# The order table of a one-core attention and gated-attention kernel is chosen anew, and every rotating buffer gets a fixed place

## The chip, the cores and the metric

The program runs on one core of one Trainium2 chip. The time is the device time of one execution in microseconds (us); three executions of the kernel before took 452.36, 452.16 and 455.88 us, median 452.36. A further execution was profiled: 453.7 us, of which the profile's span is 451.9 us.

## The reference

Two attentions follow each other. The first, for each of 8 batches and 8 heads (576 positions of 64 values), adds a local part and a coarse part. The second takes that sum as `x` and runs 4 causal attentions (experts) with a gate that keeps the best 2 of 4 at each position.

```python
q_d, k_d, v_d = means of q, k, v over 4 neighbouring positions     # 144 positions
out_up   = repeat(softmax(q_d @ k_d.T / 8) @ v_d, 4)
out_local = softmax(where(|i - j| < 4, q @ k.T / 8, -1e9)) @ v
x = (out_up + out_local) as [batch, 576, 512]
logits = x @ w_gate                                                # best 2 of 4, softmax of those
for e in range(4):
    a = softmax(causal((x @ wq[e]) @ (x @ wk[e]).T / 8))
    out += gate[e] * (a @ (x @ wv[e]) @ wo[e])
```

## The kernel before, in words

Heads go in pairs: a pair fills the 128 partitions, so a batch has 4 units of the first attention. Per unit, stage 1 loads `lq`, `lk` and `lv`, makes the local scores (`sc`, L515), masks and normalises them (`lp`), makes the coarse scores (`scd`, L588) and their softmax (`dp`), transposes both (`tp`, L383), and multiplies by the values (`o`, L650 to L662). The coarse values `vd` are means of `v`: in batch 0 TensorE makes them from `lv` with a pooling matrix (`vd_mm`, L573), later VectorE or GpSimd adds them up from a second load `lr` (L567, L568). The sum `x` is split in two parts, `xh` and `xl`, and so are all weights, so that three passes of the fast matmul type give an fp32 product.

Stage 2 projects `x` to queries, keys (`pj`, L693; the first one by pairs, L708), values and gate logits (`pv`, L739 and L748). Each of the projections of L693 is two operations, 12 matmuls of 320 columns and 12 of 256. Stage 3 makes the causal scores (`sq`, L852), the exponentials (`pr`, L875 and L883), their transposes (`tq`, L383), the product with the values (L966, L970) and the output projection (`po`, L989, L1011), which SyncE stores. Batches overlap: stage 1 of one batch, stage 2 of the one before and stage 3 of the one before that are mixed on all engines.

The mixing is written out by hand. `Plan.op` records each operation with the engines that may run it; `Plan.schedule` then goes through the table `SEQ`: an entry is four times the operation's number plus the index of the engine that runs it, and -1 is a filler, one matmul on zeros (L472) that only keeps TensorE busy. The table is thus the order of every engine's queue and the choice of engine, both. All loads and stores are issued by SyncE in the table's order. Buffers rotate by tag: `Buf.__call__` (L190) asks a tile pool for a tile of that tag with its number of buffers, and the pool picks one. The four halves of PSUM (tag `big`) are the exception: `schedule` gives them out itself, from the list `free`, at the place that was given back first.

Of the kernel before, what the change touches and what calls it, by code (L numbers as in the profile page):

```python
# [7 lines left out]
F32 = mybir.dt.float32  # L8
F32R = mybir.dt.float32r
BF = mybir.dt.bfloat16  # L10
I32 = mybir.dt.int32
# [165 lines left out]
TQ, W = 58, 64  # L177
WT, NQD = 16, 48
# [22 lines left out]
class Plan:  # L201
# [40 lines left out]
    def schedule(self):  # L242
# [8 lines left out]
        for o in out:  # L251
            for b in o.allocs:
                if b.tag == "big":
                    b.at = free.pop(0)
# [876 lines left out]
```

## Time and profile before

| | |
|---|---|
| median of three executions | 452.36 us |
| profiled execution | 453.7 us, span 451.9 us |
| TensorE busy | 441.2 us (98%) |
| VectorE busy | 362.5 us (80%) |
| ScalarE busy | 346.1 us (77%) |
| GpSimd busy | 301.2 us (67%) |
| DMA | 52.70 MB, 38.1% of the 16 engines' time |

PE is TensorE's matmuls, PEld its weight loads, DVE is VectorE, ACT ScalarE, POOL GpSimd, SP SyncE (SPq its DMA issues). Busy time is the time in which at least one instruction of the engine ran; a mean duration of a group can be longer than the engine's advance from one to the next, since neighbours overlap. "Issue" as the cause of an idle time means that the engine waited for nothing that the profile shows.

### The profile page before, as it was taken

The page shows a single profiled execution, that of the slowest core. Times are in us where ns is not written, and L with a number is a line of the kernel's source. Part 1 is how long each engine was busy: PE and PEld are TensorE (multiplying, and loading weights), DVE is VectorE, ACT ScalarE, POOL GpSimd, SP SyncE. Part 2 cuts the span into 40 slices and gives each one's busy share as a digit, 9 for nine tenths or more (in the row PEclk, how much of TensorE's full clock was granted, in tenths as well). Part 3 has the DMA queues.
Part 4 walks back from the last instruction along what each step waited for, and adds up shares of the span by engine and source line. Part 5 has one row for each costly group of instructions (what it writes and reads, how often), then busy time and mean ns, then how long its engine had stood idle before and what let it go on. Part 6 is the DMA issues. An engine that isn't in the chain of part 4 may idle for free.

```text
span 451.9 us, 20317 instructions
## 1 busy us (share of the span) xinstructions
PE 441.2 (98%) x8374; PEld 401.8 (89%) x8375; DVE 362.5 (80%) x1020; ACT 346.1 (77%) x1099; POOL 301.2 (67%) x485
## 2 busy tenths in 40 slices
PE   8998999999999999999999999999999999999997
PEld 4787999989999889998899898999999999998876
DVE  8997989896859999777988999895897768445782
ACT  7985899687968898756867888775997687456783
POOL 6997878768867888665764776765984863304320
PEclk9998999999999999999999999999999999999999
DMA  8966537433344544543334432443272200200113
GB/s 251 281 191 188 169 99 212 123 112 83 89 141 137 155 126 136 158 141 89 113 108 160 118 99 65 133 140 92 62 220 63 70 1 4 80 28 14 52 57 106
DMA packets 44300, 52.70 MB, mean 117 GB/s; under 512 B 4144, under 2 KB 27184, under 8 KB 44208
## 3 DMA queue, kind: packets, MB, share of 16 engines
q1 hardware_dynamic: 44208, 51.40, 38.1%
q8 instruction: 66, 1.08, 1.0%
q14 instruction: 26, 0.21, 0.1%
HBM read 40.90 MB, written 9.44 MB: 111 GB/s over the span
## 4 chain that ended last, share of the span: by engine, by line
PE 87%; DVE 4%; DMA 4%; issue 2%; SPq 1%; ACT 1%; DVEq 0%; ACTq 0%
PE pj L693 20%; PE pv L739 10%; PE po L989 10%; PE sq L852 9%; PE o L966 8%; PE tq L383 6%; PE tp L383 5%; PE sc L515 4%; PE o L650 4%; PE scd L588 3%; DMA lv<-in_v_dram 3%; PE pv L748 2%; PE o L657 2%; PE po L1011 1%; PE o L970 1%
## 5 line engine op out<-in xcount | busy, mean ns | idle before, releaser
L875 ACT ACTIVATE pr<-pr,pst 128x384 f32<-128x384 f32 (+8 forms) x144 | 80.0, 558 | 13.3 <-DVE pst L872 12.6
L883 POOL TENSOR_SCALAR pr<-pr,pst,gt 128x64 f32<-128x64 f32 (+8 forms) x97 | 65.9, 687 | 16.2 <-DVE pst L880 12.0
L693 PE MATMUL pj<-xh,wqk_h 128*128 128x320 f32 (+1 forms) x248 | 74.8, 302 | 0.0
L693 PE MATMUL pj<-xh,wqk_l 128*128 128x320 f32 (+1 forms) x248 | 72.8, 293 | 0.0
L693 PE MATMUL pj<-xl,wqk_h 128*128 128x320 f32 (+1 forms) x248 | 72.7, 293 | 0.0
L872 DVE CUSTOM_DVE_ANT_0 pr<-sq,causal_t 128x384 f32<-128x384 f32 (+8 forms) x144 | 63.8, 484 | 5.2 <-PE sq L852 4.7
L852 PE MATMUL sq<-k,q 64*64 64x256 f32 (+6 forms) x768 | 52.2, 370 | 0.0
L693 PEld LDWEIGHTS pj<-xh,wqk_h 128*128 128x128 f32 x248 | 46.5, 188 | 2.5 <-issue 0.6
L693 PEld LDWEIGHTS pj<-xh,wqk_l 128*128 128x128 f32 x248 | 46.5, 188 | 0.0
L693 PEld LDWEIGHTS pj<-xl,wqk_h 128*128 128x128 f32 x248 | 46.5, 187 | 0.0
L978 POOL TENSOR_TENSOR ol<-oc,oh 128x256 fp32r<-128x256 f32 (+1 forms) x27 | 22.1, 822 | 32.4 <-ACT oh L977 22.6
L852 PEld LDWEIGHTS sq<-k,q 64*64 64x64 f32 x768 | 32.9, 133 | 7.0 <-issue 0.3
L598 ACT ACTIVATE dp<-scd,dst 128x144 f32<-128x144 f32 x96 | 35.2, 376 | 3.4 <-DVE dst L593 2.7
L739 PE MATMUL pv<-wvg_h,xh 128*128 128x260 f32 x128 | 37.0, 289 | 0.0
L739 PE MATMUL pv<-wvg_l,xh 128*128 128x260 f32 x128 | 36.1, 282 | 0.0
L739 PE MATMUL pv<-wvg_h,xl 128*128 128x260 f32 x128 | 36.1, 282 | 0.0
L676 POOL TENSOR_TENSOR xl<-x,xh 128x576 fp32r<-128x576 f32 x22 | 32.4, 1473 | 4.5 <-ACT xh L675 4.0
L536 POOL TENSOR_TENSOR lp<-lp,lst 128x640 f32<-128x640 f32 x24 | 31.9, 1336 | 4.4 <-DVE lst L535 3.7
L383 PE MATMUL tq<-ident,pr 64*128 64x64 f32 x736 | 33.2, 228 | 1.4 <-DVE pst L872 0.6
L989 PE MATMUL po<-oh,wo_h 128*128 128x256 f32 (+1 forms) x112 | 34.0, 304 | 0.0
L989 PE MATMUL po<-oh,wo_l 128*128 128x256 f32 (+1 forms) x112 | 33.0, 294 | 0.0
L383 PEld LDWEIGHTS tq<-ident,pr 64*128 64x128 f32 x736 | 27.1, 138 | 6.5 <-issue 2.6
(182 smaller groups left out, 1438.8 us busy)
## 6 DMA issues: line engine op xcount, KB each, us to landing
lv<-in_v_dram SPq DMA_DIRECT2D x64, 160.0 KB, 3.7
lq<-in_qT_dram SPq DMA_DIRECT2D x32, 292.0 KB, 3.5
lk<-in_kT_dram SPq DMA_DIRECT2D x32, 292.0 KB, 3.9
out_dram<-ot SPq DMA_DIRECT2D x28, 288.0 KB, 2.3
lr<-in_v_dram SPq DMA_DIRECT2D x28, 256.0 KB, 3.2
lr<-in_v_dram SPq DMA_DIRECT2D x56, 32.0 KB, 3.0
wst<-in_wqk_dram SPq DMA_DIRECT2D x1, 1024.0 KB, 9.1
vx<-vg SPq DMA_DIRECT2D x8, 128.0 KB, 2.6
```

Source lines behind the costliest of these rows:

```text
L383: T.transpose(ps()[:, 512 * x + z[x]:512 * x + z[x] + 64], data[r, 0:128], ident[r, r])
L536: op("l_nrm", "GV", (pool_tt(n), dve(n)), lambda e: eng[e].tensor_tensor(p(), p(), st[:, :, 2:3].to_broadcast([128, NT, W]), op=OP.mult), ...
L598: A.activation(p()[:, t, :], scs()[:, at * t:at * t + SD], AF.Exp, bias=st[:, t, 4:5], scale=1.0 / 128.0, accum_out=st[:, t, 0:1])
L676: op("xl", "GV", (1360, dve(576)), lambda e: eng[e].tensor_tensor(xl(), x(), xh()[:, 0:S].bitcast(F32), op=OP.subtract), r=[x, (xh, 0)], w ...
L693: T.matmul(ps()[:, H0 + n0:H0 + n1], ww[:, c, w0 + 128 * p:w0 + 128 * p + 128], xx[b, c]()[:, n0:n1], start=(i == 0), stop=(i == 3 * NP - 1))
L739: T.matmul(ps()[:, at:at + 260], xx[b, c]()[:, 128 * t:128 * t + 128], ww[:, c, :], start=(i == 0), stop=(i == 3 * NP - 1))
L852: T.matmul(pss[x][0]()[halves[e ^ turned(t)], at_of[x] + at + to:at_of[x] + at + to + n1 - n0], q()[r, 64 * t:64 * t + 64], k()[r, n0:n1], ...
L872: op("s_max", "V", dve(n) + 4, lambda x=x, t=t, n=n, src=src: V.tensor_tensor_reduce(rows_of[t], src(), causal_t[:, S - 64:S + 256] if t = ...
L875: op("s_exp", "A", 281 + n / 1.2, lambda x=x, t=t, n=n: A.activation(rows_of[t], rows_of[t], AF.Exp, bias=st[:, x, 4:5], scale=-1.0, accum ...
L883: op("s_nrm", "GV", (327 + n / 1.2 + max(0, n - 384) * 1.1, 189 + n / 1.92), lambda g, x=x, t=t, n=n: eng[g].tensor_scalar(rows_of[t], row ...
L966: T.matmul(obs[x]()[r, q0:q1], vg()[kr, j, 64 * (2 * p + e):64 * (2 * p + e) + 64], pt()[kr, e, j, q0:q1], start=j == 0, stop=j == len(job ...
L989: T.matmul(ps()[:, H1 + n0:H1 + n1], ww[:, p, 128 * c:128 * c + 128], xx[b, p]()[:, n0:n1], start=(i == 0), stop=(i == 5))
```

## The change

The diff has two parts. In the first, every rotating buffer is treated as `big` was: `schedule` keeps a list of free places for each tag, takes the first of it at an allocation and appends a place when its last user has passed, all in the table's order; `Buf.__call__` then asks for a tag with the place's number and one buffer. The constants that are made ahead of the plan name their places too (`up0`, `qd1`, ...).

```diff
-            tag, bufs = (f"big{self.at}", 1) if self.tag == "big" else (self.tag, self.bufs)
-            self.t = self.pool.tile(self.shape, self.dtype, name=self.name, tag=tag, bufs=bufs)
+            self.t = self.pool.tile(self.shape, self.dtype, name=self.name, tag=f"{self.tag}{self.at}", bufs=1)
...
-        free = [1, 2, 3, 0]
+        free = {}
         for o in out:
             for b in o.allocs:
-                if b.tag == "big":
-                    b.at = free.pop(0)
+                b.at = free.setdefault(b.tag, list(range(b.bufs))).pop(0)
             for b in o.bufs:
                 b.left -= 1
-                if b.left == 0 and b.tag == "big":
-                    free.append(b.at)
+                if b.left == 0:
+                    free[b.tag].append(b.at)
...
-    wu = psB.tile([128, 1024], F32, name="wu", tag="big0", bufs=1)
+    wu = psB.tile([128, 1024], F32, name="wu", tag="big3", bufs=1)
```

In the second part the table is another one. It has the same 2562 operations and the same 24 fillers, and its planner counted longer delays for the arrival of instruction blocks. Line numbers after the first hunk fall by 1 or 2.

```diff
 SEQ = (
-    0, 173, 2112, 4, 177, 24, 136, 140, 189, -1, 192, 197, 120, 268, -1, 124, 232, -1, -1, -1, -1, -1, 200, 20,
...
+    214, -1, 156, 160, 288, 292, -1, -1, -1, -1, 296, 220, 8, 417, 12, 180, 164, 168, 73, 185, 320, 324, 248, 216,
...
```

Three places show what the new table moves. The first is TensorE's queue in the first batch, at the third head pair's output; `o` is its accumulator, `pv` the mean values of the fourth pair. Before:

```order
L650 MATMUL o_759<-pt,lv 64x58 x16
L650 MATMUL o_759<-pt,lv 64x56 x4
L573 MATMUL pv<-lv,pool 128x128 x7
L657 MATMUL o_759<-pd,vd 64x144 x4
L660 MATMUL o_759<-pd,vd 64x2x48
L662 MATMUL o_759<-pd,vd 64x48
```

The same place in the change:

```order
L648 MATMUL o_769<-pt,lv 64x58 x16
L648 MATMUL o_769<-pt,lv 64x56 x4
L655 MATMUL o_769<-pd,vd 64x144 x4
L658 MATMUL o_769<-pd,vd 64x2x48
L660 MATMUL o_769<-pd,vd 64x48
L658 MATMUL o_769<-pd,vd 64x2x48
L660 MATMUL o_769<-pd,vd 64x48
L571 MATMUL pv<-lv,pool 128x128 x7
```

The seven long matmuls of `pv` stand behind the short ones of `o` now, not between them.

The second place is the start of SyncE's queue, with the semaphores that each issue waits for (`DMAHW0` to `DMAHW7` are those of the eight DMA lanes that the issues take in turn, `Pool` is GpSimd). Before, from the sixth issue on:

```order
L489 DMA lk_317<-in_kT_dram 128x584
L499 DMA lv_324<-in_v_dram 64x5x128 x2
L488 DMA lq_333<-in_qT_dram 128x584 [waits DMAHW0_49]
L489 DMA lk_405<-in_kT_dram 128x584 [waits DMAHW1_49]
L499 DMA lv_431<-in_v_dram 64x5x128 [waits DMAHW2_49]
L499 DMA lv_431<-in_v_dram 64x5x128 [waits DMAHW3_49]
L488 DMA lq_434<-in_qT_dram 128x584 [waits DMAHW4_49]
L455 DMA wst_527<-in_wqk_dram 128x4x512 [waits DMAHW5_49]
```

In the change:

```order
L494 DMA lr0_95<-in_v_dram 16x512 [waits Pool_49]
L487 DMA lk_324<-in_kT_dram 128x584
L497 DMA lv_326<-in_v_dram 64x5x128
L497 DMA lv_326<-in_v_dram 64x5x128 [waits DMAHW0_49]
L486 DMA lq_363<-in_qT_dram 128x584 [waits DMAHW1_49]
L487 DMA lk_432<-in_kT_dram 128x584 [waits DMAHW2_49]
L486 DMA lq_434<-in_qT_dram 128x584 [waits DMAHW3_49]
L453 DMA wst_519<-in_wqk_dram 128x4x512 [waits DMAHW4_49]
L494 DMA lr1_96<-in_v_dram 16x512 [waits DMAHW5_49,Pool_49]
L497 DMA lv_531<-in_v_dram 64x5x128 [waits DMAHW6_49]
L497 DMA lv_531<-in_v_dram 64x5x128 [waits DMAHW7_49]
```

A small load `lr0`, which needs a tile that GpSimd has filled with zeros, is sixth now, and the second pair's `lv` has moved behind the large weight load `wst`.

The third place is VectorE's queue in batch 6, where it makes the mean values `vd` of the second pair; `oc` is the sum of an output of stage 3. Before:

```order
L327 COPY pd_5987<-tp_5974 128x480
L521 TENSOR_REDUCE lst1_70<-lp_5947 128x10
L676 TENSOR_TENSOR xl_6079<-x_5863,xh_5894 128x576
L567 TENSOR_TENSOR lr1_96<-lr1_96 128x2x256
L568 TENSOR_TENSOR vd_6098<-lr1_96 128x256
L975 TENSOR_TENSOR oc_6102<-o2_6066,oc_6102 128x192
```

In the change:

```order
L973 TENSOR_TENSOR oc_5944<-o2_5921,oc_5944 128x320
L516 SCALAR_TENSOR_TENSOR lp_5952<-sc_5879,lmask_136 128x640
L565 TENSOR_TENSOR lr1_96<-lr1_96 128x2x256
L566 TENSOR_TENSOR vd_5957<-lr1_96 128x256
L881 TENSOR_SCALAR pr20_131<-pr20_131,pst2_77,gt_5984 128x192
L519 TENSOR_REDUCE lst1_70<-lp_5952 128x10
L676 TENSOR_TENSOR xh_5950<-x_5908,xh_5950 128x64
L528 TENSOR_TENSOR lp_5952<-lp_5952,lst1_70 128x640
L325 COPY ptb_6032<-tq_6070 128x2x4x64
```

The two additions for `vd` stand earlier, and the sum `oc` of 192 columns that stood just behind them comes several instructions later.

## Rows read from the trace of the kernel before

**Rows 1.** The page: busy time by engine; 40 slices of PE, PEclk.

```profile
PE 441.2 (98%) x8374; PEld 401.8 (89%) x8375; DVE 362.5 (80%) x1020; ACT 346.1 (77%) x1099; POOL 301.2 (67%) x485
...
PE   8998999999999999999999999999999999999997
...
PEclk9998999999999999999999999999999999999999
```

**Rows 2.** Stretches: length, busy time (instructions) by engine, clock, DMA share, GB/s.

```profile
16.65:37.99 21.34, 17.96 (x525) 15.82 (x525) 18.60 (x40) 19.53 (x64) 20.74 (x25) 1.00 0.76 208
37.99:44.23 6.24, 6.24 (x109) 5.94 (x108) 4.65 (x8) 1.81 (x4) 3.62 (x6) 0.73 0.72 204
39.20:42.60 3.40, 3.40 (x30) 3.18 (x30) 2.93 (x6) 0.78 (x2) 1.45 (x2) 0.50 0.93 281
44.23:441.70 397.47, 395.17 (x7464) 364.60 (x7459) 322.49 (x928) 307.13 (x977) 263.15 (x413) 1.00 0.35 104
```

**Rows 3.** Timeline of PE at two stops: start, length, instruction, idle before.

```profile
21.70 0.40 PE L383 MATMUL tp<-ident,lp 64*128 64x64 f32 x5
23.17 0.40 PE L383 MATMUL tp<-ident,lp 64*128 64x64 f32 x5 [1.07 <-issue]
...
35.27 0.56 PE L515 MATMUL sc<-lk,lq 64*64 64x64 f32 x21
37.50 0.56 PE L515 MATMUL sc<-lk,lq 64*64 64x64 f32 x19 [1.68 <-issue]
```

**Rows 4.** Stretches as Rows 2, from the first stop's end to the second.

```profile
23.10:37.40 14.30, 12.30 (x378) 11.19 (x378) 12.24 (x28) 13.64 (x44) 13.78 (x17) 1.00 0.71 199
```

**Rows 5.** The page's DMA queues: packets, MB, share of 16 engines.

```profile
q8 instruction: 66, 1.08, 1.0%
```

**Rows 6.** Timeline of PE around the second stop, as Rows 3.

```profile
30.70 1.83 PE L573 MATMUL pv<-lv,pool 128*128 128x128 f32 x14
32.46 0.47 PE L657 MATMUL o<-pd,vd 64*64 64x144 f32 x8
...
33.02 0.52 PE L383 MATMUL tp<-ident,lp 64*128 64x64 f32 x10
33.38 0.48 PE L383 MATMUL tp<-ident,dp 64*128 64x64 f32 x10
33.78 0.71 PE L588 MATMUL scd<-kd,qd 64*64 64x144 f32 x12
34.28 0.81 PE L650 MATMUL o<-pt,lv 64*64 64x58 f32 x40
34.90 0.43 PE L657 MATMUL o<-pd,vd 64*64 64x144 f32 x8
...
37.99 0.42 PE L708 MATMUL pj<-xh,wqk_h 128*128 128x320 f32 x1
...
38.90 0.31 PE L708 MATMUL pj<-xh,wqk_h 128*128 128x320 f32 x1
...
40.08 0.47 PE L708 MATMUL pj<-xh,wqk_h 128*128 128x320 f32 x1
...
41.65 0.79 PE L383 MATMUL tp<-ident,lp 64*128 64x64 f32 x10
```

**Rows 7.** Chain that ended last, in order of time: start, length, what.

```profile
49.92 3.17 PE pj L693 x24
...
60.58 1.96 PE pj L693 x12
...
63.31 1.61 PE pj L693 x12
```

**Rows 8.** Timeline of DVE and PE at 270 us.

```profile
270.23 0.86 DVE L676 TENSOR_TENSOR xl<-x,xh 128x576 fp32r<-128x576 f32 x1
271.77 1.00 DVE L567 TENSOR_TENSOR lr<-lr 128x512 f32<-128x512 f32 x1 [0.69 <-DMA lr<-in_v_dram]
272.81 1.38 DVE L568 TENSOR_TENSOR vd<-lr 128x256 f32<-128x256 f32 x1
274.11 0.34 DVE L975 TENSOR_TENSOR oc<-o,oc 128x192 f32<-128x192 f32 x1
...
274.51 0.81 PE L515 MATMUL sc<-lk,lq 64*64 64x64 f32 x40 [0.78 <-DVE oc L975]
```

**Rows 9.** Groups of DVE instructions: shapes xcount, busy us, mean ns, idle before.

```profile
L883 DVE TENSOR_SCALAR pr<-pr,pst,gt 128x576 f32<-128x576 f32 (+7 forms) x47 | 22.4, 491 | 0.7
L551 DVE TENSOR_REDUCE qd<-lq 128x144 f32<-128x576 f32 x19 | 13.9, 731 | 0.1
L568 DVE TENSOR_TENSOR vd<-lr 128x256 f32<-128x256 f32 x11 | 7.3, 666 | 0.4
L334 DVE TENSOR_REDUCE pst<-pst 128x2 f32<-128x4 f32 (+1 forms) x47 | 7.0, 151 | 3.0 <-ACT pr L875 2.8
L327 DVE COPY vg<-pv 128x520 f32<-128x520 f32 x2 | 1.4, 698 | 0.2 <-PE pv L739 0.2
```

**Rows 10.** Stretches of 40 us, as Rows 2.

```profile
40.00:80.00 40.00, 40.00 (x824) 37.58 (x823) 36.34 (x97) 33.78 (x109) 32.70 (x45) 0.97 0.56 168
...
240.00:280.00 40.00, 38.58 (x912) 35.25 (x908) 37.70 (x99) 33.09 (x104) 27.73 (x45) 1.00 0.40 117
```

**Rows 11.** Timeline: GpSimd's preamble; SPq's issues.

```profile
2.82 1.00 POOL L372 TENSOR_SCALAR causal_t<-ci 64x64 bf16<-64x64 int32 x2
...
3.05 0.51 SPq L489 DMA_DIRECT2D lk<-in_kT_dram  x1
...
6.57 1.26 SPq L499 DMA_DIRECT2D lv<-in_v_dram  x2
9.76 0.38 SPq L455 DMA_DIRECT2D wst<-in_wqk_dram  x1
...
20.05 1.72 PE L573 MATMUL pv<-lv,pool 128*128 128x128 f32 x14
```

**Rows 12.** The page's DMA issues: KB each, us to landing.

```profile
wst<-in_wqk_dram SPq DMA_DIRECT2D x1, 1024.0 KB, 9.1
```

More of the change, by code (lines that the diff above doesn't have):

```diff
@@ L298, in tile_attn_then_moe @@
     cst = ctx.enter_context(tc.tile_pool(name="cst", bufs=1))
-    ld = ctx.enter_context(tc.tile_pool(name="ld", bufs=2))
-    wk = ctx.enter_context(tc.tile_pool(name="wk", bufs=2))
+    ld = ctx.enter_context(tc.tile_pool(name="ld", bufs=1))
+    wk = ctx.enter_context(tc.tile_pool(name="wk", bufs=1))
     psB = ctx.enter_context(tc.tile_pool(name="psB", bufs=1, space=bass.MemoryType.PSUM))
@@ L357, in tile_attn_then_moe @@
     V.memset(zero, 0.0)
-    wu = psB.tile([128, 1024], F32, name="wu", tag="big0", bufs=1)
+    wu = psB.tile([128, 1024], F32, name="wu", tag="big3", bufs=1)
     for _ in range(NW0):
         T.matmul(wu[:, 0:512], zero[:, :128], zero, start=True, stop=True)
-    ci = wk.tile([128, 128], I32, name="ci", tag="up")
+    ci = wk.tile([128, 128], I32, name="ci", tag="up0")
     G.iota(ci, pattern=[[1, 128]], base=0, channel_multiplier=-1)
-    cj = wk.tile([128, 128], I32, name="ci", tag="up")
+    cj = wk.tile([128, 128], I32, name="ci", tag="up1")
     G.iota(cj, pattern=[[1, 128]], base=64, channel_multiplier=-1)
-    cut = wk.tile([128, 5, WT], I32, name="cut", tag="qd")
+    cut = wk.tile([128, 5, WT], I32, name="cut", tag="qd0")
     for x, r in enumerate(halves):
@@ L372, in tile_attn_then_moe @@
         G.tensor_scalar(causal_t[x, 512:S], c[x, 0:64], 0.0, 8 * NEG, op0=OP.is_gt, op1=OP.mult)
-    dif2, far = (wk.tile([128, W], F32, name=n, tag=t) for n, t in (("dif", "qd"), ("far", "kd")))
+    dif2, far = (wk.tile([128, W], F32, name=n, tag=t) for n, t in (("dif", "qd1"), ("far", "kd0")))
     for x, c in ((lo, ci), (hi, cj)):
         V.tensor_copy(dif2[x], c[x, 0:64])
-    near = wk.tile([128, W], F32, name="near", tag="kd")
+    near = wk.tile([128, W], F32, name="near", tag="kd1")
     V.tensor_scalar(near, dif2, 0.0, None, op0=OP.is_lt)
@@ L409, in tile_attn_then_moe @@
         V.scalar_tensor_tensor(own[:, x:x + 1], dif2[:, 0:1], -PADL - n + 0.5, own[:, 1:2], op0=OP.is_gt, op1=OP.mult)
-    inside = wk.tile([128, 5, WT], F32, name="inside", tag="vt", bufs=1)
+    inside = wk.tile([128, 5, WT], F32, name="inside", tag="vt0")
     for k0, k1 in ((0, 4), (4, 5)):
```

280 rows, old and new, of the table SEQ are left out of this document.

## The prediction, on record before the run

> **What bounds the kernel now.** I read the page first, then stretches of the span, then the timeline where TensorE stands still. The page says that TensorE's matmuls are busy for 441.2 of 451.9 us and that no slice from the second to the 39th is below eight tenths [rows 1]. The stretches say where the rest is: from 44.23 to 441.70 us PE is busy for 395.17 of 397.47 us, so 397 us of the span hold 2.3 us of visible idle time; from 16.65 to 37.99 us it is busy for 17.96 of 21.34, and behind that the clock falls [rows 2]. The reader should see that this kernel is one TensorE queue with almost no holes. The other engines have at most 80% and matter only where one of them releases a matmul late. Whatever the new table does, it has the same matmuls and the same 24 fillers to run, so it can gain the holes of the first 44 us, the 2.3 us behind them, and small losses at the joints between operations.
>
> **The first part of the change: places.** It costs nothing by itself. I compared the addresses in the program before with a list kept as the change keeps it, first back first taken, over before's own order: of 723 takings of SBUF buffers, some 12 would get another place (6 of `ot`, 2 each of `pt`, `oc` and `dp`). PSUM was given out this way already. So no wait of any weight goes or comes with the places, and the table is the change.
>
> **Term 1, instruction blocks at the head.** TensorE stops twice inside an operation, without any wait: 1.07 us in the middle of ten transposes and 1.68 us in the middle of the 40 local scores [rows 3]. Between the end of the first and the start of the second stand 378 matmuls and 378 weight loads, 756 instructions [rows 4]; with some dozen waits of the sequencer, which that view does not count, this is 768, three times 256. The instruction queue q8 moved 66 packets with 1.08 MB, 16.4 KB each [rows 5], for 8374 + 8375 = 16,749 such instructions [rows 1], 254 a packet. So I read each stop as the start of a packet's instructions that had not arrived. The head is where it can happen: a local score is 40 matmuls and their loads in 0.81 us [rows 8], a pooling (L573) 14 of each in 1.83 us [rows 6].
> The new table moves the last pooling behind the short output matmuls, as the first order piece shows. Counted back from the 1.68 us stop, with a weight load for each matmul, stand 42 instructions of the scores, 32 of the coarse output, 80 of the local output, 24 coarse scores and 40 for two transposes [rows 3, 6]: 218, so some 35 of the packet's 256 are left, the waits taken off. Before, these are the 32 of the coarse output (32.46 to 33.02, 0.56 us) and a few of the pooling; now they are the pooling's 28 (30.70 to 32.46, 1.76 us) and a few of the coarse output [rows 6]. The packet that ends in the stop thus gets 1.0 us more of work to cover the next one's arrival. But the pooling is taken from the packet ahead, which has that much less: the later stop loses some 1.0 us, and 0.5 may come back one packet earlier. I take **-0.5**. The ends: -2.75, if both stops vanish, and +1.07, if one more of the first kind appears.
> On the rule: the Trainium skill, page "Runtime: NRT & Kernel Launch", section "Instruction fetch mechanics", says that instructions come in blocks of 16 KiB, 256 instructions, and that crossing a boundary is mostly hidden because dispatch is slower than the fill. The trace agrees with the size and differs on the hiding: two stops of 1.07 and 1.68 us. By that rule this term would be zero, and so the next.
>
> **Term 2, the clock.** After the second stop the granted clock is 0.50 for 3.40 us, from 39.20 to 42.60, which is 1.2 instead of 2.4 GHz [rows 2]. The first six projection matmuls take 0.91 us (37.99 to 38.90), the twelve after that 2.75 (to 41.65) instead of 1.82 [rows 6]: 0.93 us. The stop of 1.07 us was not followed by such a fall; the stretch from 16.65 to 37.99 has 1.00 [rows 2, 3]. If the second stop shrinks from 1.68 to about 0.7, it is shorter than the one that did no harm. I take **-0.9**; the ends are -0.93 and 0.
>
> **Term 3, joints.** A projection whose two halves follow each other takes 3.17 us; with transposes between them the halves take 1.96 and 1.61, 3.57 in sum [rows 7]. Before, 10 of the query and key projections of L693 are split; now 7. Three joints at 0.2 (half of the 0.40, since the rows' ends are modelled) are **-0.6**; the ends are -1.2 and 0.
>
> **Term 4, VectorE behind a load.** At 271.08 VectorE waits 0.69 us for `lr`, then adds for 2.3 us, and `oc`, next in its queue, comes so late that TensorE stands for 0.78 us [rows 8]. The third order piece moves the additions ahead and puts other work between them and that `oc`. Behind the waiting instruction now stand a normalisation and a maximum of stage 1, whose readers are on other engines. That stop goes, -0.8; but in batch 4 the new table puts three `lr` pieces directly ahead of VectorE's additions, which the old one does not. I take **-0.4**; the ends are -0.8 and +0.8.
>
> **Term 5, VectorE has more to do.** 83 operations go from GpSimd to VectorE and 73 the other way, 45 from ScalarE to VectorE and 33 back. By kinds, VectorE's net gains are 7 normalisations (0.49 us), 8 sums of `qd` and `kd` (0.73), 3 `vd` (0.67 for each of two additions), some 11 evictions (0.70 at most), 3 `o_lo` and 5 `xt`; it loses 11 small sums (0.15), 4 passes over `lp` and one `xl` [rows 9]. With each kind's own mean that is about +16.5 us by durations; durations overlap, so busy time grows by some 15, to 377 of the span, 83%. GpSimd loses about 17. Spread evenly it is 1.3 us in each 40. In the one 40 us stretch behind the head in which VectorE has 37.70, TensorE was idle for 1.42; at 36.34 it was idle for none [rows 10]. So one more stretch, the one at 36.34, comes to 37.7. Half of 1.42 is **+0.7**. The ends are 0 (all of it in VectorE's free time) and +15 (all of it on the path).
>
> **Term 6, loads at the head.** SyncE's sixth issue now waits for GpSimd's zeroed tile. GpSimd is in its preamble until 3.82 and a fill follows, so about 4.3 instead of 3.05 [rows 11]; five earlier transfers are still on their way, so I cost it at nothing. The second `lv` is issued behind the 1 MB weight load, which landed at 9.76 + 9.1 = 18.9 [rows 11, 12]; TensorE asked for that `lv` at 20.05. About a microsecond is left, so **0**; the ends are 0 and +1.
>
> **The sum.** -0.5 - 0.9 - 0.6 - 0.4 + 0.7 = -1.7 us against the profiled execution's 453.7, 452.0 under the profiler. That execution is 1.3 above the median of 452.36; against the median it is 450.7 us. The case's own range, with terms 1, 2 and 4 at either end, is 448.0 to 454.3.
>
> **The rivals.**
> *Blocks don't matter, the head stays as it is.* The stops are of another cause, or spread over other packets at the same sum, and the clock falls as before. Terms 3 to 5 remain: -0.3, **452.1 us**. For it: the dense stretch as a whole holds the same work, only cut otherwise. This is also what the rule of the Trainium skill named above would make of the head. Against it: the 768 instructions between the stops.
> *All stops go.* Both stops, the clock and the 2.3 us behind 44 us: -2.75 - 0.93 - 2.3 - 0.6 = -6.6, **445.8 us**. For it: the table is chosen for longer block delays, and the dense packets later on are thinned too. Against it: the fillers stay and the head's work per packet stays.
> *VectorE becomes the bound.* If its extra work falls into stretches that are full already, half of the 15 us lands on TensorE: +7.5 and terms 1 to 3 at half, -1.0: **458.9 us**. It decides where VectorE passes 37.7 of 40 us in three or more stretches, and TensorE's idle releaser is VectorE. For it: 37.70 in one stretch already. Against it: mean room of 20%.
>
> **How the numbers follow.** Forecast 0.50, head as before 0.22, all stops go 0.15, VectorE bound 0.13. About 1% (4.5 us) is what a measurement here tells from no change. The forecast's own range and the second case lie within it; the third is faster and the fourth slower, and I leave 0.02 of the forecast to each side. Faster 0.17, same 0.68, slower 0.15. Predicted is 450.7; the range takes in the faster case's near half and stops short of the slower one: 446.5 to 457.
>
> **What would show it.** Term 1: the issue stops of PE in the first 40 us, 2.75 in sum, should be about 2.2, none above 1.1. Term 2: no 0.50 clock near 40 us. Term 3: query and key projections with 24 matmuls in one piece, more by three. Term 4: no `DMA lr` wait on VectorE ahead of an `oc` near 270. Term 5: VectorE about 377 us, GpSimd about 285, and PE still idle for under 4 us from 44 us on. Term 6: no PE idle with the second `lv` as releaser. The prediction is wrong if PE's busy time between 44 and 441 us changes by more than 3 us, since nothing above speaks of that.

## The result, and the profile after

The change makes the kernel slower by about half a per cent: 456.86 us, median of 20 executions (454.95 to 461.99), beside 454.21 for the kernel before (also 20 executions); the ratio is 1.0057, 95% interval [1.0038, 1.0077], so 2.6 us with 1.7 to 3.5. The prediction had said 1.7 us faster. The profiled execution of the changed kernel took 454.95 us, the fastest of its 20, so its head is a lucky one; a more usual execution of the same table is profiled below (second run of the experiments).

The page of the changed kernel, busy time, TensorE and its clock in 40 slices:

```profile
PE 442.0 (98%) x8375; PEld 401.0 (88%) x8375; DVE 376.3 (83%) x1054; ACT 341.0 (75%) x1089; POOL 278.5 (61%) x457
...
PE   8989999999999999999899999999999999999997
...
PEclk9999999999999999999999999999999999999999
```

VectorE has 13.8 us more than in [rows 1], GpSimd 22.7 less. Next the stretches, as [rows 2, 10]:

```profile
37.99:44.23 6.24, 6.17 (x165) 5.66 (x165) 5.61 (x11) 4.73 (x16) 5.42 (x8) 1.00 0.73 237
44.23:441.70 397.47, 394.28 (x7386) 363.30 (x7387) 335.36 (x957) 300.79 (x963) 242.37 (x390) 1.00 0.35 103
...
80.00:120.00 40.00, 39.03 (x832) 35.44 (x834) 36.76 (x107) 32.46 (x104) 27.13 (x43) 1.00 0.39 113
200.00:240.00 40.00, 38.61 (x667) 35.98 (x666) 37.33 (x99) 28.19 (x90) 18.82 (x35) 1.00 0.39 114
240.00:280.00 40.00, 40.00 (x928) 36.84 (x928) 35.58 (x101) 32.57 (x102) 28.62 (x46) 1.00 0.43 125
```

In this execution the clock does not fall behind 38 us. The loss of TensorE's busy time sits in two stretches (0.97 and 1.39 us idle), and the stretch from 240 to 280, which idled 1.42 us before, is full now. What TensorE waited for (total us, times, longest):

```profile
PE tq L381 <- DVE pr L881: 1.9, 2, 1.4
...
PE o L660 <- issue: 0.9, 1, 0.9
...
PE sq L850 <- DVE ptb L325: 0.6, 1, 0.6
PE pv L571 <- issue: 0.5, 1, 0.5
PE pj L691 <- DVE x L668: 0.4, 1, 0.4
PE sc L513 <- issue: 0.4, 1, 0.4
```

Three new waits for VectorE, and smaller "issue" stops than in [rows 3]. To see where the time goes I took the start of each TensorE operation in two traces and subtracted. Negative is earlier than in the profiled execution before (us); "new table" is the second run below, "old table" the first:

| at | changed kernel | new table, usual execution | old table, another execution |
|---|---|---|---|
| 56 | -0.8 | +0.75 | +0.4 |
| 110 | +0.7 | +2.3 | +0.4 |
| 190 | +0.8 | +2.3 | +0.6 |
| 240 | +2.6 | +4.0 | +0.6 |
| 300 | +0.9 | +2.3 | +0.6 |
| 435 | +1.3 | +2.8 | +1.25 |

The head differs from execution to execution. The body hardly does (the old table's second execution loses 0.4 us at 344 without a wait): both executions of the new table lose 1.5 us between 56 and 110, 1.7 to 1.8 between 190 and 240, and gain 1.7 between 240 and 300. The place at 220 us, VectorE and GpSimd from 215.4 to 220.6, by form (busy us, mean ns):

```profile
L976 DVE TENSOR_TENSOR ol<-oc,oh 128x320 fp32r<-128x320 f32 x1 | 1.7, 1699 | 0.0
L674 POOL TENSOR_TENSOR xl<-x,xh 128x576 fp32r<-128x576 f32 x1 | 1.6, 1626 | 0.0
L881 DVE TENSOR_SCALAR pr<-pr,pst,gt 128x576 f32<-128x576 f32 x1 | 1.5, 1547 | 0.0
...
L528 POOL TENSOR_TENSOR lp<-lp,lst 128x640 f32<-128x640 f32 x1 | 1.4, 1403 | 0.0
L553 POOL TENSOR_TENSOR dh<-lk 128x288 f32<-128x288 f32 x1 | 0.9, 913 | 0.0
L881 DVE TENSOR_SCALAR pr<-pr,pst,gt 128x384 f32<-128x384 f32 x1 | 0.8, 816 | 0.0
```

The same in time (start, length):

```profile
216.04 1.40 POOL L528 TENSOR_TENSOR lp<-lp,lst 128x640 f32<-128x640 f32 x1
217.41 1.63 POOL L674 TENSOR_TENSOR xl<-x,xh 128x576 fp32r<-128x576 f32 x1
218.99 0.91 POOL L553 TENSOR_TENSOR dh<-lk 128x288 f32<-128x288 f32 x1
...
215.91 1.86 DVE L881 TENSOR_SCALAR pr<-pr,pst,gt 128x256 f32<-128x256 f32 x2
217.68 1.70 DVE L976 TENSOR_TENSOR ol<-oc,oh 128x320 fp32r<-128x320 f32 x1
219.30 1.27 DVE L881 TENSOR_SCALAR pr<-pr,pst,gt 128x384 f32<-128x384 f32 x2
...
220.18 0.46 PE L381 MATMUL tq<-ident,pr 64*128 64x64 f32 x8 [1.39 <-DVE pr L881]
```

Each VectorE instruction ends a few tenths behind the end of a GpSimd instruction that ran beside it: 217.77 behind 217.44, 219.38 behind 219.04, 220.12 behind 219.90. They take turns. TensorE stands for 1.39 us. At 79 us the same: `vd` takes 1.41 us, where it takes 0.42 without GpSimd beside it (below), while GpSimd's `wlo` takes 1.74, and `x`, next on VectorE, is late by the difference, some 1.0 us:

```profile
78.36 1.74 POOL L459 TENSOR_TENSOR wo_l<-wst,wo_h 128x512 fp32r<-128x512 f32 x1
...
78.97 1.41 DVE L566 TENSOR_TENSOR vd<-lr 128x256 f32<-128x256 f32 x1
80.30 0.74 DVE L668 SCALAR_TENSOR_TENSOR x<-up,o 128x576 f32<-128x576 f32 x1
...
81.19 0.39 PE L691 MATMUL pj<-xh,wqk_h 128*128 128x320 f32 x1 [0.42 <-DVE x L668]
```

"Excess" below is the time from an operation's start to the next one's beyond its usual value: 0.58 us at 79, 0.78 at 86, 1.65 at 218; in the kernel before 0.68 at 253 and 1.00 at 273. An excess is good to some 0.1 us.

### The profile page after: what moved, and what is told of

It is laid out like the page before. It is cut to its first block, busy times and chain, and to the rows that moved or that the text cites. A ratio compares the mean times of both kernels' runs of the same rounds, so it can differ in the third digit from the quotient of the medians.

```text
span 453.2 us, 20298 instructions
## 1 busy us (share of the span) xinstructions
PE 442.0 (98%) x8375; PEld 401.0 (88%) x8375; DVE 376.3 (83%) x1054; ACT 341.0 (75%) x1089; POOL 278.5 (61%) x457
## 3 DMA queue, kind: packets, MB, share of 16 engines
q8 instruction: 66, 1.08, 1.0%
## 4 chain that ended last, share of the span: by engine, by line
PE 86%; DVE 9%; issue 1%; ACT 1%; DMA 1%; POOL 1%; SPq 0%; ACTq 0%; DVEq 0%; POOLq 0%
PE pj L691 20%; PE po L987 10%; PE pv L737 10%; PE sq L850 9%; PE o L964 7%; PE tq L381 5%; PE tp L381 4%; PE sc L513 4%; PE o L648 3%; PE scd L586 3%; PE pv L746 2%; PE pv L571 2%; PE o L655 2%; PE po L1009 1%; DMA lk<-in_kT_dram 1%
## 5 line engine op out<-in xcount | busy, mean ns | idle before, releaser
L873 ACT ACTIVATE pr<-pr,pst 128x320 f32<-128x320 f32 (+8 forms) x144 | 80.0, 560 | 15.8 <-DVE pst L870 14.8
L881 POOL TENSOR_SCALAR pr<-pr,pst,gt 128x448 f32<-128x448 f32 (+8 forms) x90 | 57.4, 643 | 28.0 <-DVE pst L878 23.4
L870 DVE CUSTOM_DVE_ANT_0 pr<-sq,causal_t 128x256 f32<-128x256 f32 (+8 forms) x144 | 63.6, 485 | 12.4 <-PE sq L850 11.8
L976 POOL TENSOR_TENSOR ol<-oc,oh 128x256 fp32r<-128x256 f32 (+1 forms) x24 | 19.7, 822 | 32.9 <-ACT oh L975 32.8
L534 POOL TENSOR_TENSOR lp<-lp,lst 128x640 f32<-128x640 f32 x26 | 34.1, 1312 | 7.3 <-DVE lst L533 4.9
L323 ACT COPY ptb<-tq 128x384 f32<-128x384 f32 (+4 forms) x71 | 29.9, 484 | 5.8 <-PE tq L381 5.6
L987 PE MATMUL po<-ol,wo_h 128*128 128x256 f32 (+1 forms) x112 | 33.1, 295 | 0.0
```

The costliest lines, as they stand in the source:

```text
L534: op("l_nrm", "GV", (pool_tt(n), dve(n)), lambda e: eng[e].tensor_tensor(p(), p(), st[:, :, 2:3].to_broadcast([128, NT, W]), op=OP.mult), ...
L870: op("s_max", "V", dve(n) + 4, lambda x=x, t=t, n=n, src=src: V.tensor_tensor_reduce(rows_of[t], src(), causal_t[:, S - 64:S + 256] if t = ...
L873: op("s_exp", "A", 281 + n / 1.2, lambda x=x, t=t, n=n: A.activation(rows_of[t], rows_of[t], AF.Exp, bias=st[:, x, 4:5], scale=-1.0, accum ...
L881: op("s_nrm", "GV", (327 + n / 1.2 + max(0, n - 384) * 1.1, 189 + n / 1.92), lambda g, x=x, t=t, n=n: eng[g].tensor_scalar(rows_of[t], row ...
L987: T.matmul(ps()[:, H1 + n0:H1 + n1], ww[:, p, 128 * c:128 * c + 128], xx[b, p]()[:, n0:n1], start=(i == 0), stop=(i == 5))
```

## The experiments

**Places or table.** The two halves of the change apart.

```diff
 e1_places: after's code   SEQ = that of before
 e2_table:  before's code  SEQ = that of after
```

> The fixed places alone: the changed kernel's way of giving out buffers, with the table of the kernel before. Theory A (the loss is in the table's new choice of engines: operations moved from GpSimd to VectorE run long beside GpSimd and release TensorE late) and theory B (the loss is in the new order of the queues) both expect no change, ratio 0.998 to 1.002, and TensorE's stops at the same times as before (23.2, 37.5, 253 and 273 us). Theory C (the places cost: an operation waits for its fixed place) expects the whole loss here, about +2.6 us or 1.006.

Measured 455.53 us, ratio 1.002 [0.9992, 1.0049].

> The new table alone, with the kernel before's way of giving out buffers. A and B: the whole loss, +2.6 us, ratio 1.004 to 1.008, with a stop of TensorE of over 1 us near 218 us that follows a normalisation of VectorE. C: no loss, or even the head's gain of 0.9 us.

Measured 457.02 us, ratio 1.0054 [1.0028, 1.008]. The table carries the loss; the places are not told from nothing. The profile of the second has the three stops at the same operations (excess 0.55, 0.78, 1.70), and a worse head:

```profile
PE o L656 <- issue: 2.0, 1, 2.0
PE tq L377 <- DVE pr L877: 2.0, 2, 1.5
```

**Order or engines.** The new table's order with the old choice of engines, and the reverse (241 operations differ).

> The changed kernel, but every operation runs on the engine that it had before: the new order alone. A: the loss goes and the gains of the head (0.9 us by 54 us) and of the stop at 273 us stay, 1 to 2 us faster than before, ratio 0.995 to 0.999, VectorE busy for about 362 us again. B: as slow as the changed kernel, 1.004 to 1.008.

> The kernel before, but every operation runs on the engine that the new table gives it: the new choice of engines alone, in the old order. A: slower by 1 to 4 us, ratio 1.002 to 1.009, VectorE busy for about 376 us and TensorE waiting for VectorE where a normalisation or an o_lo of VectorE runs beside GpSimd. B: no change, 0.998 to 1.002.

Measured 497.27 us (1.0927) and 509.81 us (1.1232). Both theories miss: order and engines fit only each other. A mixture waits all along (in the second TensorE is busy for 142.7 of the 160 us from 40 to 200), so the two runs decide nothing about the loss.

**The instructions by themselves.**

> A kernel of its own, which computes nothing of the reference: four forms of VectorE instruction, five times each, alone and beside GpSimd's tensor_tensor of 128x576 (two SBUF inputs), tensor_scalar of 128x576 and memset of 128x576. A: the tensor_scalar on SBUF and the tensor_tensor with two SBUF inputs advance one by one with GpSimd's instructions, some 1.4 us each beside the tensor_tensor instead of 0.4; the tensor_tensor with one input from PSUM changes less, and the tensor_reduce not at all. D: all take the same time alone and beside GpSimd, within 0.1 us.

VectorE's forms alone and beside GpSimd's two-input `tensor_tensor`, five of each (busy us, mean ns):

```profile
L50 DVE TENSOR_SCALAR vo<-a,s 128x576 f32<-128x576 f32 x5 | 2.4, 540 | 0.0
...
L41 POOL TENSOR_TENSOR go<-ga,gb 128x576 f32<-128x576 f32 x5 | 7.8, 1595 | 0.1
L50 DVE TENSOR_SCALAR vo<-a,s 128x576 f32<-128x576 f32 x5 | 6.8, 1411 | 0.0
...
L52 DVE TENSOR_TENSOR vo<-a,b 128x320 f32<-128x320 f32 x5 | 2.1, 486 | 0.0
...
L52 DVE TENSOR_TENSOR vo<-a,b 128x320 f32<-128x320 f32 x5 | 8.0, 1665 | 0.0
...
L54 DVE TENSOR_TENSOR vo<-ps,b 128x320 f32<-128x320 f32 x5 | 2.1, 483 | 0.0
...
L41 POOL TENSOR_TENSOR go<-ga,gb 128x576 f32<-128x576 f32 x5 | 6.8, 1402 | 0.1
...
L56 DVE TENSOR_REDUCE vo<-a 128x9 f32<-128x576 f32 x5 | 3.5, 748 | 0.0
...
L56 DVE TENSOR_REDUCE vo<-a 128x9 f32<-128x576 f32 x5 | 3.5, 746 | 0.0
```

The first and second pair are alone, then beside GpSimd: 540 to 1411 ns (the first of its five ran ahead; the others took 1.53 to 1.65 us) and 486 to 1665. With one input from PSUM (L54) the time beside GpSimd is 483, as alone, and GpSimd keeps its 1402; `tensor_reduce` keeps 746. GpSimd loses too, 1402 to 1595. Beside GpSimd's `tensor_scalar` VectorE's `tensor_scalar` takes 0.97 to 1.08 us (the first ran ahead), but the two-input `tensor_tensor` its usual 0.48 in three of five and 0.95 in two; beside GpSimd's `memset` the `tensor_tensor` keeps 0.49, and the `tensor_scalar` takes 0.56 to 1.17. So how long VectorE is held depends on what GpSimd runs. The Trainium skill, page "SBUF — State Buffer", section "Who interferes with whom", says the same: VectorE's `copy` and `tensor_scalar` in their two-port mode, and its instructions with two SBUF inputs, share a port pair with GpSimd, whoever starts first keeps it for the whole instruction, and `tensor_reduce` never contends on this chip. The trace agrees, with these numbers.

**More work on VectorE, none beside it on GpSimd.** If the hold makes the stop, VectorE with more to do is faster there.

```diff
-    ... 5652, 5656, 5020, ...      l_sub (5,1) and xl (4,2) on GpSimd
+    ... 5653, 5656, 5021, ...      on VectorE
```

> The changed kernel with two operations more on VectorE: the subtraction of lp (L528, 1.40 us on GpSimd at 216.04) and xl (L674, 1.63 us on GpSimd at 217.41) run on VectorE, behind the normalisations that TensorE waits for; nothing else is moved. Theory A, now sharper (an instruction of VectorE that reads or writes SBUF in its fast form, or reads two SBUF tensors, cannot run while GpSimd works on SBUF tensors, so the two alternate): with GpSimd empty there, the normalisations and o_lo take 0.4 to 0.5 us each instead of 0.8 to 1.7, TensorE's stop of 1.4 us at 218.8 goes, and the time is 1.4 us less than the changed kernel's, 1.001 to 1.004 of before, though VectorE has 1.5 us more to do. Theory D (VectorE has too much to do): the stop stays or grows, 1.005 to 1.009.

Measured 456.98 us, ratio 1.0059 [1.0031, 1.0087]. The same instructions by form, and TensorE:

```profile
L875 DVE TENSOR_SCALAR pr<-pr,pst,gt 128x576 f32<-128x576 f32 x1 | 0.6, 576 | 0.0
...
L970 DVE TENSOR_TENSOR ol<-oc,oh 128x320 fp32r<-128x320 f32 x1 | 0.5, 487 | 0.0
...
220.57 1.20 PE L375 MATMUL tq<-ident,pr 64*128 64x64 f32 x32
...
225.30 0.46 PE L580 MATMUL scd<-kd,qd 64*64 64x144 f32 x6 [1.11 <-DVE pst L864]
```

1547 became 576 ns, 1699 became 487, and the 32 transposes run in one piece. But the 1.5 us that VectorE took over now stand ahead of its maxima, and TensorE waits for those, 1.11 us (excess 1.19). So the hold made the stop at 218, as A said; that VectorE has no room behind it is theory D's point, and it holds as well. The time did not fall: it is in D's range and not in A's. (From 56 to 435 us this execution loses 1.7 us against the kernel before, the two of the new table 2.15 and 2.0.)

```diff
 e6_three: as e5_lock218, and
-    ... 1748, 116, 1700, ...            wlo on GpSimd
+    ... 1748, 117, 1700, ...            on VectorE
-    ... 2945, ... 1921, ...             kd (3,0), then ptb (0,0,3)
+    ... 1921, 2945, ...                 ptb first
```

> As the run before, and two edits more: one wlo (L459, 1.74 us on GpSimd at 78.36, beside which vd of VectorE takes 1.41 instead of 0.42) runs on VectorE; and the copies ptb of VectorE at 86.36 stand ahead of the sums kd of the next unit (0.85 us), not behind them. A: the stops at 80.8 and 87.2 go as well, excess there 0.58 and 0.78 us, so about 3 us less than the changed kernel, 0.998 to 1.001 of before. D: VectorE has over 2 us more to do than in the changed kernel and the time is no better than 1.004.

Measured 455.93 us, 1.0031 [1.0007, 1.0055]: the stop at 80.8 is gone (`vd` 0.43 us), that at 87.2 became one of 0.40 for `oc` two operations later (excess 0.60, not 0.78). About 1 us came back of the 3 that A expected, and the interval overlaps that of the changed kernel.

**The stops of the kernel before.**

> The kernel before with two edits at its own two stops: the normalisation of lp at 251.10, which takes 2.07 us on VectorE beside xl of GpSimd, runs on GpSimd instead; and vd of batch 6 (L567 and L568, 271.77 to 274.19, of which 1.4 us beside GpSimd's additions of the same kind) stands behind the two maxima that follow it. A: the stops of 0.60 at 254.1 and 0.78 us at 273.7 go, 1.4 to 1.7 us less than before, ratio 0.996 to 0.998. If these stops have another cause (the loads of lr, as the prediction took it), the second stays the same: 0.998 to 1.000.

The two places in the kernel before, the normalisation `lp` beside `xl`, and GpSimd's additions that run beside `vd` of [rows 8]:

```profile
251.08 1.41 POOL L676 TENSOR_TENSOR xl<-x,xh 128x576 fp32r<-128x576 f32 x1
...
251.10 2.07 DVE L536 TENSOR_TENSOR lp<-lp,lst 128x640 f32<-128x640 f32 x1
...
272.19 1.72 POOL L567 TENSOR_TENSOR lr<-lr 128x512 f32<-128x512 f32 x1
```

Measured 453.52 us, 0.9976 [0.9944, 1.0008]; in this run the next load of `lr` stood ahead of the moved additions, so one pair's `vd` was made of other values. Both stops went; the later `vd` made one of excess 0.68 at 276 and one of 0.53 behind it. The next run keeps `vd` in its place:

```diff
-    ... 6256, 6261, 5600, ...      l_nrm (5,3) on VectorE
+    ... 6256, 6260, 5600, ...      on GpSimd
-    ... 6676, 6724, 5908, 5912,    vd (6,0) of GpSimd
+    ... 6724, 5908, 5912, 6676,    behind its next o_lo
```

> The kernel before with one edit at each of its own two stops, both of which only take GpSimd's instruction away from beside VectorE's: the normalisation of lp at 251.10 (2.07 us on VectorE beside xl of GpSimd) goes to GpSimd, and GpSimd's additions lr and vd at 272.19, beside which VectorE's vd takes 1.38 instead of 0.43, stand behind GpSimd's next o_lo, at 277. A: the stops of 0.60 at 254.1 and 0.78 at 273.7 go with nothing in their place, excess 1.7 us, ratio 0.996 to 0.998. If the second stop comes from the load of lr that VectorE waits for, as the prediction had it, it stays and the ratio is 0.998 to 1.000.

Measured 451.94 us, ratio 0.9972 [0.995, 0.9994], **faster than both kernels**, by an interval that just excludes no change. The stretch from 240 to 280, whose idle time was 1.42 us [rows 10], and VectorE at 270, as [rows 8]:

```profile
240.00:280.00 40.00, 39.99 (x926) 36.48 (x926) 35.73 (x98) 33.75 (x107) 26.99 (x45) 1.00 0.40 119
...
271.83 1.61 DVE L561 TENSOR_TENSOR lr<-lr 128x512 f32<-128x512 f32 x1
273.48 0.42 DVE L562 TENSOR_TENSOR vd<-lr 128x256 f32<-128x256 f32 x1
273.82 0.35 DVE L969 TENSOR_TENSOR oc<-o,oc 128x192 f32<-128x192 f32 x1
```

`vd` takes 0.42 us instead of 1.38, without GpSimd's additions beside it. The load of `lr` was not late in this execution, so by itself the run does not rule out the load as the cause of the second stop. Two other executions of the old table do: in e1_places VectorE waited 0.30 us for the load, in e13_load_early (below) 0.17, and TensorE's stop was still 0.76 and 0.78. The second:

```profile
273.80 1.52 DVE L561 TENSOR_TENSOR lr<-lr 128x512 f32<-128x512 f32 x1 [0.17 <-DMA lr<-in_v_dram]
...
277.06 0.81 PE L509 MATMUL sc<-lk,lq 64*64 64x64 f32 x40 [0.78 <-DVE oc L969]
```

Where the load comes earlier, VectorE's first addition is held beside GpSimd's `lp` (1.52 us here and 1.61 in e10_before_mended, 0.69 in e8_before_two without it), so the wait for the load costs nothing more. In its profiled execution (454.38 us) e10_before_mended lost some 1.0 us of what it had gained in two stops at 351 and 379 us, at borders between instruction packets, which no other profile has there.

**The head.** TensorE's instruction packets were followed from the crossing of the border before (in the head no packet started ahead of that) to the start of the transfer on q8, and to the border where the packet is needed.

> The changed kernel with two loads later in SyncE's queue, nothing else: lk of batch 2 (292 KB, issued at 27.32) behind the weights of the output projection, and lv of the third pair of batch 1 (80 KB, issued at 27.92) behind the load that followed it (30.92). Theory E (the instruction packet that TensorE stands for at 31.7 leaves late, at 30.3 to 32.1 instead of 29.5, because the DMA engines are busy with loads for 0.85 of 28 to 30 us, where the kernel before leaves them 0.14): the packet starts before 30 us, the stop of 0.91 to 3.3 us at that place is under 1.0, and the median is 0.8 to 1.5 us less than the changed kernel's, 1.002 to 1.004 of before. Theory F (the prediction's own: only the place of the packet's border in TensorE's work counts): the stop stays at 2 to 3 us, 1.005 to 1.007.

Measured 457.5 us, 1.009 [1.0064, 1.0116] from 6 executions.

> The kernel before with one load earlier in SyncE's queue: the 512 KB of weights of the output projection, issued at 38.47, stand ahead of the lq that was issued at 29.74, so they are issued at about 26 and keep the DMA engines busy until 30 or 31. There the packet that TensorE needs at 32.14 was fetched in 2.0 us after TensorE crossed the border before it (27.45), with the DMA engines at 0.37. E: it leaves 3.5 to 5 us after that, as in the changed kernel, and TensorE stops for 1.5 to 3 us near 32 us, where it did not stop before; the later stop near 36 shrinks by a part of that. Median 0 to 1.5 us above before. F: no stop near 32 us.

Measured 453.75 us, 0.9981 [0.9957, 1.0005]; the profiled execution, 456.43 us, is the slowest of its ten.

In the table, e11_mended is the run that follows this part; it has the two later loads of e9_quiet.

```
packet needed near 32 us:   border  to its start  DMA share  stop
kernel before               27.45   2.0 us        0.37       none
e1_places                   29.64   1.35          0.02       none
changed kernel              26.86   3.5           0.86       0.91
e2_table                    26.61   4.0           0.85       2.0
e6_three                    26.82   3.7           0.83       2.0
e5_lock218                  26.85   5.2           0.86       3.3
e12_body                    27.11   5.1           0.87       3.5
e9_quiet                    26.61   3.0           0.86       0.59
e11_mended                  27.12   5.5           0.95       3.6
e13_load_early              28.66   2.6           0.82       under 0.4
```

Where TensorE stopped for a packet, it went on 2.4 to 3.0 us after the transfer's start, in both tables; so a packet that starts late enough is a stop. With the new table it starts 3.0 to 5.5 us behind the border, with the old 1.35 to 2.3 (e10_before_mended 1.7, e8_before_two 2.3), with the load moved 2.6. Theory E says that loads on the DMA engines are why. The rows do not settle it. Busy DMA engines and late packets go together (2.6 to 5.5 us at 0.82 to 0.95, up to 2.3 at 0.39 or less), but nearly all the busy rows are of the new table. In e9_quiet the packet left before 30 us and the stop was under 1.0, as E forecast; but the following loads moved up, so that the engines were no emptier (0.86), the next packet was late instead (a stop of 1.83 us), and the time did not fall. e11_mended, with the same two loads moved, has a packet 5.5 us late and a stop of 3.6. In e13_load_early a load that fills the engines cost the packet 0.6 us, not 1.5 to 3. So E is not shown. F (only the place counts) is refuted by stops of 0.91 to 3.5 us at one place of one head. What delays the packet stays open.

**Mended together.** Four edits of the body and the two of e9_quiet:

> The changed kernel with the two later loads of the run beside it and four edits at its stops: the subtraction of lp at 216.04 on VectorE, behind its maxima (xl stays on GpSimd); the normalisation that TensorE waits for at 220 ahead of o_lo; wlo of 78.36 behind the small sums that follow it on GpSimd, so that vd on VectorE runs alone; and the sums kd of batch 3 (85.48 on VectorE) on GpSimd again, as in the kernel before. A and E together: the stops at 80.8, 87.2 and 218.8 go (excess 0.58, 0.78 and 1.65) and the head's stop is under 1 us: 3 to 4.5 us less than the changed kernel, 0.996 to 0.999 of before, faster than both. D: no better than 1.003.

Measured 459.02 us, 1.0131 [1.0088, 1.0174]; the profiled execution, 462.22 us, is the slowest of its six. The stop at 218 went, but TensorE stood 1.8 us for a normalisation of GpSimd at 96 us, behind which the granted clock was 0.50 for 3.4 us, and its head had a stop of 3.6. I take `kd` and `wlo`, which GpSimd got ahead of that normalisation, as the cause; it was not tried apart:

```profile
PE o L654 <- issue: 3.6, 1, 3.6
PE tq L375 <- POOL pr L875: 1.8, 1, 1.8
```

The body alone, without GpSimd's part:

```diff
 e12_body: wlo and l_sub (5,1) on VectorE, ptb before kd as in e6_three, and
-    ... 4645, 4785, 4925, ...      o_lo, then s_nrm (2,1,3)
+    ... 4785, 4645, 4925, ...
-    ... 5652, 5656, ... 5192,      l_sub, l_exp, then the maxima
+    ... 5192, 5653, 5656,
```

> The changed kernel with its head as it is and only the edits at the body's stops that held so far: wlo of 78.36 on VectorE instead of GpSimd; the copies ptb of 86.36 ahead of the sums kd; at 216 the normalisation that TensorE waits for ahead of o_lo, and the subtraction of lp on VectorE, behind the five maxima that TensorE's next operations wait for (with its exponential behind it on ScalarE). VectorE has 1.5 us more to do than in the changed kernel. A: the stops at 80.8 and 218.8 go with nothing over 0.5 us in their place, the excess over usual durations between 60 and 240 us is 2.0 us or less where the changed kernel has 5.2, and the time is 1.5 to 3 us less, 0.999 to 1.003 of before. D: as slow as the changed kernel or slower, 1.005 or more.

Measured 456.06 us, 1.0034 [1.0009, 1.0059]: about 1 us less than the changed kernel, short of the 1.5 to 3 that A expected, faster than D's 1.005, and not down to before; the interval overlaps that of the changed kernel. The stops of 80.8 and 218.8 are gone; in their place stand excesses of 0.60 at 89, 0.39 at 222 and 0.90 at 224, where TensorE waits for what VectorE has put off. `xl` is still on GpSimd here, and the normalisation of 576 columns beside it still takes 1.68 us; the stop at 218 went with one of the two held instructions that stood ahead of what TensorE waits for, `o_lo`, which now stands behind it and takes 0.48. A hold by itself is thus not yet a stop; what stands behind it has to be awaited. From 56 to 435 us this execution loses 1.2 us against the kernel before, the new table unmended 2.0 and 2.15. No mended version of the new table came back to the time of the kernel before.

## Why the prediction was wrong

**Term 5, VectorE has more to do: mis-sized, +0.7 put, about +3.0 measured.** The busy times came nearly as said (376.3 for 377, GpSimd 278.5 for 285). But I priced them by the room in 40 us, with a rival's limit at 37.7, and the stops came at 36.76 and 37.33. What counted was less how much VectorE has than what runs beside it: two of the three new stops follow an instruction of VectorE that was held by GpSimd (1.65 and 0.58 of excess; undone in e5_lock218 and e6_three), the third a full queue (0.78). In the mended runs a full queue is what took the place of the stops: 1.11 us behind VectorE's maxima in e5_lock218, 0.90 at 224 us in e12_body. [Rows 8, 9] had it: `vd` 1.38 us against a mean of 0.67, and I took the long one as given. VectorE's held time is not larger in sum than before (durations beyond the lower fifth of each form: 14.1 us in the changed kernel, 15.5 before); its places changed.

**Term 4, VectorE behind a load: -0.4 put, -1.7 measured, and for another reason.** The stop at 273 went, and so did the one at 253, which I had not costed. VectorE's `vd` and `lp` were held by GpSimd there, as e10_before_mended shows. The wait for `lr`, on which the term rests, was not the cause: with 0.17 us of it instead of 0.69 the stop was the same 0.78.

**Terms 1 and 2, the head: -1.4 put, nothing measured that can be told from zero.** In the profiled execution it came as said: stops of 0.54, 0.91 and 0.38 instead of 1.07 and 1.68, no clock of 0.50, 0.8 us earlier at 56 us. In the other four profiles of the new table with the same head the stop at 31.7 is 2.0 to 3.5 us. Their starts at 56 us, with the first, are -0.8, +0.75, +2.0, +0.3 and +2.2, mean +0.9; the old table's four with its head unchanged are 0, +0.4, +0.2 and +1.35, mean +0.5. The border moved as I counted. What failed is the step that takes the packet's arrival as fixed and covers it with work.
The clock's fall did not go: the mean granted clock was under 0.998 in 18 of 32 executions of the new table and in 70 of 110 of the old. In e2_table it is 0.73 from 33.61 to 40.00, behind the 2.0 us stop. Nor is the length of the stop, by which term 2 judged, enough to tell: in the kernel before the clock fell behind 1.68 us, in e10_before_mended it did not behind stops of 2.07 and 1.95.

**Term 3, joints.** Three more projections run in one piece (7 of the 31 of L693 split instead of 10). The 0.6 us cannot be seen: outside the three new stops and the two that went, the two executions of the new table lose 0.8 and 0.7 us from 56 to 435, where the joints should gain.

**Term 6, loads at the head.** No wait for the second `lv`; nothing, as said. **Places:** not told from nothing in e1_places, whose interval leaves up to 0.5%.

The sum, with what was measured in place of what was put: head +0.4, which is not told from zero, term 4 -1.7, term 5 +3.0, and the 0.7 to 0.8 of term 3's paragraph, which I have not explained (0.35 and 0.5 of it between 350 and 435 us): +2.4 to +2.5, within the 1.7 to 3.5. Of the rivals the third was the nearest, VectorE as the bound, but its point of decision, a share of 40 us, was the wrong one.

## What to carry to other kernels

Before moving an elementwise operation between VectorE and GpSimd, list what the other engine runs at that moment: a VectorE `tensor_scalar` on SBUF, or an instruction with two SBUF inputs, beside a two-input instruction of GpSimd costs its own time plus what is left of GpSimd's. Look first at instructions that take two or three times their form's usual time and release TensorE; separating the two engines at two such places gave 0.28% here (interval 0.06 to 0.5), where a whole new table lost 0.57%. And a head that differs by 3 us from execution to execution needs several profiles before a stop in it is credited to a change.

## What the runs showed of the hardware

A VectorE `tensor_scalar` or two-input `tensor_tensor` on SBUF and GpSimd's two-input `tensor_tensor` alternate instruction by instruction, and both lose: 540 to 1411 and 1402 to 1595 ns in the first pair; with one VectorE operand in PSUM neither does (483 and 1402). Where TensorE stood for a packet of instructions, it went on 2.4 to 3.0 us after the packet's transfer started, but the one needed near 32 us started 1.35 to 5.5 us behind the border before, and with one head 3.5 to 5.2 from execution to execution. The Trainium skill, page "Runtime: NRT & Kernel Launch", section "Instruction fetch mechanics", has such a border mostly hidden; past 44 us the traces agree (in 11 of 12 profiles no stop at a border over 0.3 us shows; e10_before_mended has two, of 0.45 and 0.31), in the head they do not.
